# A three-stage attention and expert kernel: one step of the exact weight conversion moved from VectorE to ScalarE, and the first softmax tiles done in whole-tile instructions

## The chip, the cores and the metric

The kernel runs on one core of one Trainium2 chip. The metric is the device time of one launch in microseconds; lower is better. The engines of the core are TensorE (PE, with its weight loads as PEld), VectorE (DVE), ScalarE (ACT), GpSimd (POOL) and SyncE (SP), which issues most of the transfers.

## The reference

Three parts run one after the other on 2304 tokens. Attention with keys and values averaged over 8 positions:

```python
k_p = k.reshape(B, H, Sp, 8, D).mean(axis=3)          # B, H, S, D = 4, 8, 576, 64; Sp = 72
scores = scale * np.matmul(q, k_p.transpose(0, 1, 3, 2))
attn = np.exp(scores - np.max(scores, axis=-1, keepdims=True))
attn = attn / (np.sum(attn, axis=-1, keepdims=True) + 1e-09)
out = np.matmul(attn, v_p)
```

Then a feed-forward part in float64 weights, `y = relu(x @ w_in)**2 @ w_out`, with `w_in` 512 x 2048 and `w_out` 2048 x 512. Then a routing part: each token goes to the one of 8 experts with the largest gate logit, `relu(x @ w1) @ w2`, scaled by its gate.

## The kernel before, in words

The 2304 tokens are 9 chunks of 256 (`c` from 0 to 8). For each chunk the attention makes the input `x` of the feed-forward part, in two halves: a rounded one `xh` (ScalarE) and the rest `xl` (VectorE). Each of 16 feed-forward steps of a chunk (`g1`) is: 12 matmuls into `h` (L585), a ReLU on ScalarE (`relu`, L590), a square on VectorE or ScalarE (`square`), a rounded half `gh` on ScalarE (`high`, L601), the rest `gl` on GpSimd (`low`, L605), and 6 matmuls into `y` (L618). Chunks 0 and 1 run interleaved, one step of each by turns, and the attention of chunk 2 runs beside them.

The weights of the feed-forward part come as 64-bit floats and are converted in place as they arrive, 32 tiles of 128 x 512 (`conv(i)`). A raw tile has two 32-bit words for each number: word 1 holds the sign, the exponent and the upper bits, word 0 the lower ones. The result `cv` is put together with bits alone. Before the change:

- `sign` (VectorE, L259): `cv` = the sign bit of word 1.
- `scale` (ScalarE, L263): word 1, read as a float, times a power of two, which moves the exponent's bias.
- `merge` (VectorE, L267), twice: `cv` or word 1 shifted left by 3, then `cv` or word 0 shifted right by 29 (its top three bits).
- `high` (ScalarE, L273) writes the rounded half of the tile, `low` (GpSimd, L276) the rest.

`cv` has 4 buffers; the raw tile and the finished tile share one.

A softmax tile (`a_scores`) is up to 128 rows of 8 heads by 72 keys in two halves `a` of 4 heads. There are two forms. The whole-tile form: VectorE takes the maximum (`top`), subtracts it (`less`, L420), ScalarE does one exponential for 4 heads (`exp4`, L424), VectorE sums (L456). The head-by-head form: VectorE takes the maximum and multiplies it by a negative constant (`neg`, L409), and ScalarE does one exponential for each head with the maximum as bias and its sum as a second output (`exp`, L412, two records each). Both end with a small constant added to the sums (L428) and a reciprocal (L429) on VectorE, and a product (`norm`, L433) on GpSimd, for one tile on VectorE. Before the change the whole-tile form is used for two tiles, one of chunk 0 and one of chunk 1; the other 18 tiles go head by head.

The order of the instructions on each engine is fixed by a planner (`Steps.run`): each step has a priority, an engine and a cost in nanoseconds, and the planner takes, engine by engine, the first step of a window of 80 that could start by these costs. The costs thus decide the order of the program, and nothing else. The engines then run their own lists in order.

Of the kernel before, what the change touches and what calls it, by code (L numbers as in the profile page):

```python
# [20 lines left out]
POOL = 8  # L21
# [173 lines left out]
def tile_kernel(ctx: ExitStack, tc: tile.TileContext, q, k, v, w_in, w_out, w_gate, w1, w2, cap, gate_rows, consts, out):  # L195
# [101 lines left out]
    def k_pool(b, x, prio, load_prio, tag=None):  # L297

        buf, box = Buf("kvraw" if tag is None else tag), {}

        def load():
            box["raw"] = raw_tile(tag, f"kraw_{b}_{x}")
            nc.sync.dma_start(out=box["raw"], in_=k[b, x])

        def pool():
            nc.vector.tensor_reduce(
                out=kd[:, x], in_=box["raw"].rearrange("p (s r) -> p s r", r=POOL), axis=AX.X, op=ALU.add
            )

        add(load_prio, "SP", 840, load, w=(buf,), lat=2000)  # L310
        add(prio, "DVE", 690, pool, r=(buf, "ap"), w=(("kd", x),))

    def v_pool(b, i, prio, load_prio, tag=None):
        n = min(P, NROW - i * P)
# [66 lines left out]
    def a_scores(c, j, prio, qprio):  # L381
# [18 lines left out]
        def top(a):  # L400
            if "mx" not in box:
                box["mx"] = ap.tile([P, H], F32, tag="mx", name=f"mx_{c}_{j}", bufs=2)
                box["sm"] = ap.tile([P, H], F32, tag="sm", name=f"sm_{c}_{j}", bufs=2)
                box["ex"] = a_tile([P, H, SP], "ex", c, j, 2)
            nc.vector.tensor_reduce(out=box["mx"][:n, 4 * a:4 * a + 4], in_=box["sc", a][:n], axis=AX.X, op=ALU.max)

        def neg(a):
            m = box["mx"][:n, 4 * a:4 * a + 4]
            nc.vector.tensor_scalar_mul(out=m, in0=m, scalar1=-1.0 / 64.0)  # L409

        def exp(h):
            nc.scalar.activation(  # L412
                out=box["ex"][:n, h], in_=box["sc", h // 4][:n, h % 4], func=AF.Exp, scale=1.0 / 64.0,
                bias=box["mx"][:n, h:h + 1], accum_out=box["sm"][:n, h:h + 1],
            )
# [18 lines left out]

        st["ex", c, j] = box, ex
        add(qprio, "SP", 760 * n // P, load, w=(qT,), lat=2000)
        cells, us, tags = [], [], []
        for a in range(2):
            pool, tag = (pg, "g") if c == 2 else (pp, f"y{a}") if c < 2 and j == 1 else (pp, "sc")
# [5 lines left out]
                us.append(())  # L445
            tags.append((a, pool, tag))
        for part in [tags] if c == 2 else [tags[:1], tags[1:]]:
            add(prio(2), "PE", 480 * len(part), lambda part=part: [qk(*x) for x in part], r=(qT, ("kT", 0), ("kT", 1), "kT in", "ap"),
                w=[cells[x[0]] for x in part], u=us[part[0][0]])
        if c in DVE_SOFTMAX and (c, j) not in ACT_SOFTMAX:  # L450
            for a in range(2):
                w, u = (cells[a],), us[a]
                add(prio(3), "DVE", 370, lambda a=a: top(a), r=w, w=((mxb, a),), u=(*u, mxb, ex))
                add(prio(3), "DVE", 360, lambda a=a: less(a), r=(*w, (mxb, a)), w=((ex, a),), u=(*u, mxb, ex))
                add(prio(3), "ACT", 350, lambda a=a: exp4(a), w=((ex, a),), u=(ex,))
            add(prio(4), "DVE", 620, lambda: nc.vector.tensor_reduce(  # L456
                out=box["sm"][:n], in_=box["ex"][:n], axis=AX.X, op=ALU.add), r=((ex, 0), (ex, 1)), w=((mxb, 2),), u=(mxb, ex))
# [114 lines left out]
    def g1(c, ff, prio):  # L572
# [59 lines left out]
        add(prio + 5, "PE", 1310, mm2, r=(ghb, glb, ("W", 16 + ff, 0), ("W", 16 + ff, 1)), w=(("y", c),), u=yb)
# [909 lines left out]
```

## Time and profile before

| what | value |
|---|---|
| time, median of 3 runs | 789.33 us (787.2 to 789.95) |
| the profiled execution's time | 788.33 us |
| its span | 786.2 us, so 2.1 us lie around the span |
| TensorE busy | 702.9 us, 89% of the span |
| VectorE busy | 455.5 us, 58% |
| ScalarE busy | 317.9 us, 40% |
| GpSimd busy | 242.7 us, 31% |
| mean granted TensorE clock | 0.947 of full speed |

The shares are means over stages with different limits. The weight conversion runs from about 15 to 140 us; from there to about 540 us TensorE hardly pauses; then come the experts. The line of the profile that cuts the span into 40 slices shows this: one slice is 19.7 us.

### The profile page before, as it was taken

Reading aid. Unit: us, or ns where it says so; the run is one execution under the profiler, and the core shown is the slowest. Engines: PE = TensorE matmul, PEld = TensorE weight load, DVE = VectorE, ACT = ScalarE, POOL = GpSimd, SP = SyncE. Lnnn points to the kernel's source line nnn. Section 1 sums busy time; section 2 is a strip of 40 time slices with the busy share of each in tenths; the row PEclk is TensorE's granted clock in tenths of the full one; section 3 lists DMA queues with packets and bytes.
Section 4 is the critical chain, followed back from the end, with each engine's and each line's share of the span. In section 5 each row is a group of like instructions: output and inputs, shape, how many; then the busy total and the mean of one; then the engine's idle time right before and its main releaser. Section 6 shows DMA issues by size and latency. Waiting matters only on the chain. (4 is left out here: it accounts for less than half of the span.)

```text
span 786.2 us, 12381 instructions
## 1 busy us (share of the span) xinstructions
PE 702.9 (89%) x4231; PEld 616.0 (78%) x4232; DVE 455.5 (58%) x1181; ACT 317.9 (40%) x950; POOL 242.7 (31%) x267
## 2 busy tenths in 40 slices
PE   4788888999999999999999999997969669979993
PEld 4568676899898888888988998995949568868872
DVE  6999999322279896282696474453514412625371
ACT  3755655444343334344333433443113412624360
POOL 4476586323134233233132332221020112010240
PEclk9599999999999999999999999998888979989997
DMA  9926763210031310010100000600062611636261
GB/s 328 405 89 198 245 186 103 61 68 14 15 135 56 103 42 8 8 41 15 39 15 6 28 1 26 244 2 29 2 229 89 222 46 37 202 100 200 80 200 56
DMA packets 42597, 78.06 MB, mean 99 GB/s; under 512 B 8673, under 2 KB 18145, under 8 KB 42336
## 3 DMA queue, kind: packets, MB, share of 16 engines
q1 hardware_dynamic: 39888, 68.56, 25.9%
q0 software_dynamic: 2576, 7.93, 3.2%
q8 instruction: 58, 0.95, 0.6%
q14 instruction: 75, 0.61, 0.3%
HBM read 63.57 MB, written 13.44 MB: 98 GB/s over the span
## 5 line engine op out<-in xcount | busy, mean ns | idle before, releaser
L585 PE MATMUL h<-xh,W 128*128 128x256 f32 x1152 | 220.0, 289 | 3.1 <-DVE r L597 2.9
L605 POOL TENSOR_TENSOR gl<-r,gh 128x256 fp32r<-128x256 f32 x144 | 117.1, 814 | 277.7 <-ACT gh L601 189.6
L585 PEld LDWEIGHTS h<-xh,W 128*128 128x128 f32 x1152 | 186.3, 193 | 17.1 <-DVE r L597 6.5
L618 PE MATMUL y<-W,gh 128*128 128x512 f32 x576 | 187.9, 407 | 0.8 <-POOL W L276 0.8
L585 PE MATMUL h<-xl,W 128*128 128x256 f32 x576 | 163.7, 284 | 2.6 <-DVE xl L524 2.6
L597 DVE SCALAR_TENSOR_TENSOR r<-h,r 128x256 f32<-128x256 f32 x141 | 59.0, 418 | 112.5 <-ACT r L590 112.5
L618 PE MATMUL y<-W,gl 128*128 128x512 f32 x288 | 114.6, 398 | 0.1
L618 PEld LDWEIGHTS y<-W,gh 128*128 128x128 f32 x576 | 100.0, 191 | 17.3 <-issue 1.5
L585 PEld LDWEIGHTS h<-xl,W 128*128 128x128 f32 x576 | 111.0, 193 | 2.8 <-DVE xl L524 2.8
L1255 PE MATMUL hp<-yh,W 128*128 128x256 f32 (+1 forms) x384 | 83.7, 315 | 31.1 <-issue 31.1
L590 ACT ACTIVATE r<-h 128x256 f32<-128x256 f32 x144 | 55.2, 384 | 108.6 <-PE h L585 96.1
L601 ACT CAST gh<-r 128x256 fp32r<-128x256 f32 x144 | 58.8, 408 | 98.1 <-DVE r L597 89.9
L1255 PEld LDWEIGHTS hp<-yh,W 128*128 128x128 f32 x384 | 68.0, 210 | 36.0 <-issue 35.9
L1224 PE MATMUL po<-W,hh 128*128 128x512 f32 x224 | 71.1, 399 | 0.0
L675 DVE SCALAR_TENSOR_TENSOR junk<-ysb,wgb 128x512 bf16<-128x512 f32 x80 | 64.5, 806 | 1.9 <-ACT ysb L648 0.4
L618 PEld LDWEIGHTS y<-W,gl 128*128 128x128 f32 x288 | 54.6, 190 | 13.8 <-POOL gl L605 1.0
L267 DVE SCALAR_TENSOR_TENSOR cv<-raw,cv 128x512 int32<-128x512 int32 x64 | 62.9, 1008 | 0.4 <-ACT raw L263 0.3
L1255 PE MATMUL hp<-yl,W 128*128 128x256 f32 (+1 forms) x192 | 59.6, 311 | 2.2 <-issue 2.2
L1261 DVE SCALAR_TENSOR_TENSOR hl<-hp,hh 128x256 fp32r<-128x256 f32 x48 | 20.1, 422 | 59.6 <-ACT hh L1260 58.4
L514 PE MATMUL av<-aT,vz 128*128 128x256 f32 (+3 forms) x192 | 47.2, 379 | 8.1 <-DVE xl L524 5.5
L1213 POOL DMA_INDIRECT out_dram<-ysb,sidx x16 | 16.4, 1024 | 121.0 <-ACT ysb L1202 87.4
L276 POOL TENSOR_TENSOR W<-cv,W 128x512 fp32r<-128x512 f32 x32 | 46.4, 1459 | 21.5 <-ACT W L273 16.8
(185 smaller groups left out, 975.6 us busy)
## 6 DMA issues: line engine op xcount, KB each, us to landing
stg<-in_moe_w_dram SPq DMA_DIRECT2D x47, 512.0 KB, 4.8
raw<-in_moe_w_in_dram SPq DMA_DIRECT2D x16, 512.0 KB, 7.1
raw<-in_moe_w_out_dram SPq DMA_DIRECT2D x16, 512.0 KB, 7.4
kraw<-in_k_dram SPq DMA_DIRECT2D x16, 288.0 KB, 3.6
out_dram<-zt SPq DMA_DIRECT2D x18, 256.0 KB, 3.7
y_dram<-ysb SPq DMA_DIRECT2D x18, 256.0 KB, 2.4
qT<-in_q_dram SPq DMA_DIRECT2D x16, 256.0 KB, 3.2
vraw<-in_v_dram SPq DMA_DIRECT2D x16, 256.0 KB, 3.4
```

The costliest lines, as they stand in the source:

```text
L267: nc.vector.scalar_tensor_tensor(out=a, in0=box["raw"][:, :, word], scalar=shift, in1=a, op0=op, op1=ALU.bitwise_or)
L276: nc.gpsimd.tensor_tensor(out=W[i][:, 1], in0=f(box["a"]), in1=f(W[i][:, 0]), op=ALU.subtract)
L514: nc.tensor.matmul(ps[:, :n], vz[:m, cm].rearrange("p r d -> p (r d)"), abox["aT"][:m, blk, :n], start=(x == 0), stop=(x == 1),)
L585: nc.tensor.matmul(ps, wt[kk][:, l, o:o + P], r[:, kk, :], start=(n == 0), stop=(n == 3 * KD - 1))
L590: nc.scalar.activation(out=box["r"], in_=box["ps"], func=AF.Relu)
L597: nc.vector.scalar_tensor_tensor(out=r, in0=box["ps"], scalar=0.0, in1=r, op0=ALU.max, op1=ALU.mult)
L601: nc.scalar.copy(out=box["gh"], in_=box["r"])
L605: nc.gpsimd.tensor_tensor(out=box["gl"], in0=box["r"], in1=f(box["gh"]), op=ALU.subtract)
L618: nc.tensor.matmul(st["y", c][t], l[:, ts], r, start=(ff == 0 and n == 0), stop=(ff == NF - 1 and n == 2))
L675: nc.vector.scalar_tensor_tensor(out=junk, in0=st["yb", c, t] if c < 2 else st["ysb", c][t], scalar=1.0, in1=st["wgb"][:, e], op0=ALU.mult ...
L1224: nc.tensor.matmul(ps, l, r, start=(fi == 0 and x == 0), stop=(fi == 7 and x == 2))
L1255: nc.tensor.matmul(ps, ww[:, l, o], r[:, kk, 0:n2], start=(kk == 0 and x == 0), stop=(kk == KD - 1 and x == 2))
```

## The change

The conversion of a weight tile: `sign` is gone. A new ScalarE step `last` (L260 of the changed kernel) reads the upper 16 bits of word 0 as an unsigned integer, and scale, bias and the conversion to an integer on output leave its top three bits in `cv`. `scale` follows on ScalarE as before. VectorE then does two merges (L270), both from word 1: first the sign bit (an AND), then the shift by 3. So a tile has three VectorE instructions before and two after, and two ScalarE ones before `high` instead of one.

The softmax: all 7 tiles of chunks 0, 1 and 2 take the whole-tile form. The factor 1/64 of the scores moves into the copy that places the pooled keys (`k_place`, L347), which is an activation with a scale instead of a copy. The maximum comes out of `top` negated, so `neg` is gone everywhere. The small constant is added on ScalarE (`guard`, L427) and no more on VectorE.

The first matmuls of chunk 2's attention also depend on the last `xl` of chunk 1 (`after`). Many planner costs are changed, which moves instructions on all engines.

```diff
-DVE_SOFTMAX = (0, 1)
-ACT_SOFTMAX = ((0, 1), (1, 0))
+DVE_SOFTMAX = (0, 1, 2)
+ACT_SOFTMAX = ()
...
-        def sign():
+        def last():
+
             a = box["a"] = tp.tile([P, 512], I32, tag="cv", name=f"cv{i}", bufs=4)
-            hw = box["raw"][:, :, 1]
-            nc.vector.tensor_scalar(out=a, in0=hw, scalar1=-0x80000000, scalar2=None, op0=ALU.bitwise_and)
+            nc.scalar.activation(
+                out=a, in_=box["raw"].bitcast(U16)[:, :, 1], func=AF.Copy, scale=2.0 ** -13, bias=2.0 ** -14 - 0.5
+            )
...
-        def merge(word, shift, op):
+        def merge(x, op):
             a = box["a"]
-            nc.vector.scalar_tensor_tensor(
-                out=a, in0=box["raw"][:, :, word], scalar=shift, in1=a, op0=op, op1=ALU.bitwise_or
-            )
+            nc.vector.scalar_tensor_tensor(out=a, in0=box["raw"][:, :, 1], scalar=x, in1=a, op0=op, op1=ALU.bitwise_or)
...
-        add(prio, "DVE", 340, sign, r=(raw, "tp"), w=(cv,))
-        add(prio, "ACT", 520, scale, w=(raw,))
-        add(prio, "DVE", 605, lambda: merge(1, 3, ALU.logical_shift_left), r=(raw,), w=(cv,))
-        add(prio, "DVE", 605, lambda: merge(0, 29, ALU.logical_shift_right), r=(raw,), w=(cv,))
-        add(prio, "ACT", 525, high, r=(cv,), w=(("W", i, 0),), u=(whole,))
-        add(prio, "POOL", 1225, low, r=(cv, ("W", i, 0)), w=(("W", i, 1),))
+        add(prio, "ACT", 650, last, r=(raw, "tp"), w=(cv,))
+        add(prio, "ACT", 680, scale, w=(raw,))
+        add(prio, "DVE", 1000, lambda: merge(-0x80000000, ALU.bitwise_and), r=(raw,), w=(cv,))
+        add(prio, "DVE", 1000, lambda: merge(3, ALU.logical_shift_left), r=(raw,), w=(cv,))
+        add(prio, "ACT", 620, high, r=(cv,), w=(("W", i, 0),), u=(whole,))
+        add(prio, "POOL", 1460, low, r=(cv, ("W", i, 0)), w=(("W", i, 1),))
...
-            nc.scalar.copy(out=pairs[h, :, a], in_=kd[h])
+            nc.scalar.activation(out=pairs[h, :, a], in_=kd[h], func=AF.Copy, scale=1.0 / 64.0)
...
-            nc.vector.tensor_reduce(out=box["mx"][:n, 4 * a:4 * a + 4], in_=box["sc", a][:n], axis=AX.X, op=ALU.max)
-
-        def neg(a):
-            m = box["mx"][:n, 4 * a:4 * a + 4]
-            nc.vector.tensor_scalar_mul(out=m, in0=m, scalar1=-1.0 / 64.0)
+            nc.vector.tensor_reduce(
+                out=box["mx"][:n, 4 * a:4 * a + 4], in_=box["sc", a][:n], axis=AX.X, op=ALU.max, negate=True
+            )
...
+        def guard():
+            sm = box["sm"]
+            nc.scalar.activation(out=sm[:n], in_=sm[:n], func=AF.Copy, bias=1e-9)
+
         def recip():
             sm = box["sm"]
-            nc.vector.tensor_scalar_add(out=sm[:n], in0=sm[:n], scalar1=1e-9)
             nc.vector.reciprocal(out=sm[:n], in_=sm[:n])
...
+        after = [("xl", 1, 0, NPAIR - 1)] if c == 2 else []
```

Three places of the instruction order carry the prediction. The first is ScalarE at the start of the program, up to the first transposed attention tiles `aT`; `ex` are exponentials, `cv0` and `raw0` belong to weight tile 0. Before, the first line stands twice more for the second half of the tile:

```order
L412 ACTIVATE ex_0_1_158,sm_0_1_157<-sc_0_1_1_152,mx_0_1_156 128x72 x4
L263 ACTIVATE raw0_148<-raw0_148 128x512
L263 ACTIVATE raw1_168<-raw1_168 128x512
L273 CAST W0_223<-cv0_189 128x512
L490 COPY aT_0_0_231<-ata_0_0_214 128x4x128
L493 COPY aT_0_0_231<-atb_0_0_229 64x128
```

And after:

```order
L423 ACTIVATE ex_0_1_157<-ex_0_1_157 128x288
L427 ACTIVATE sm_0_0_134<-sm_0_0_134 128x8
L260 ACTIVATE cv0_183<-raw0_148 128x512
L423 ACTIVATE ex_0_1_157<-ex_0_1_157 128x288
L266 ACTIVATE raw0_148<-raw0_148 128x512
L260 ACTIVATE cv1_198<-raw1_166 128x512
L427 ACTIVATE sm_0_1_156<-sm_0_1_156 128x8
L266 ACTIVATE raw1_166<-raw1_166 128x512
L493 COPY aT_0_0_217<-ata_0_0_204 128x4x128
L496 COPY aT_0_0_217<-atb_0_0_213 64x128
```

The copy of `aT` stood behind the second `scale`, which waits for a VectorE `sign`; now the rows ahead of it that belong to weights wait for transfers alone, and the only VectorE results in front of it are those of the softmax.

The second place is VectorE in the same part of the program, the end of chunk 0's softmax and the first weight tiles. Before:

```order
L428 TENSOR_SCALAR sm_0_1_157<-sm_0_1_157 128x8
L429 RECIPROCAL sm_0_1_157<-sm_0_1_157 128x8
L433 TENSOR_TENSOR ex_0_1_158<-ex_0_1_158,sm_0_1_157 128x576
L267 SCALAR_TENSOR_TENSOR cv0_189<-raw0_148,cv0_189 128x512
L259 TENSOR_SCALAR cv1_210<-raw1_168 128x512
L267 SCALAR_TENSOR_TENSOR cv0_189<-raw0_148,cv0_189 128x512
L259 TENSOR_SCALAR cv2_221<-raw2_185 128x512
L267 SCALAR_TENSOR_TENSOR cv1_210<-raw1_168,cv1_210 128x512
```

And after:

```order
L270 SCALAR_TENSOR_TENSOR cv0_183<-raw0_148,cv0_183 128x512
L431 RECIPROCAL sm_0_1_156<-sm_0_1_156 128x8
L270 SCALAR_TENSOR_TENSOR cv0_183<-raw0_148,cv0_183 128x512
L435 TENSOR_TENSOR ex_0_1_157<-ex_0_1_157,sm_0_1_156 128x576
L270 SCALAR_TENSOR_TENSOR cv1_198<-raw1_166,cv1_198 128x512
L406 TENSOR_REDUCE mx_1_0_242<-sc_1_0_0_163 128x4
L270 SCALAR_TENSOR_TENSOR cv1_198<-raw1_166,cv1_198 128x512
```

The signs between the merges are gone, and with them the small addition ahead of the reciprocal.

The third place is ScalarE in the middle of the conversion, at weight tiles 22, 23 and 8. Before:

```order
L263 ACTIVATE raw22_454<-raw22_454 128x512
L263 ACTIVATE raw23_487<-raw23_487 128x512
L263 ACTIVATE raw8_518<-raw8_518 128x512
L590 ACTIVATE r_0_4_706<-h_0_4_667 128x256
L590 ACTIVATE r_1_3_718<-h_1_3_689 128x256
L601 CAST gh_0_4_723<-r_0_4_706 128x256
```

And after:

```order
L260 ACTIVATE cv22_690<-raw22_381 128x512
L604 CAST gh_1_3_695<-r_1_3_678 128x256
L266 ACTIVATE raw22_381<-raw22_381 128x512
L274 CAST W21_712<-cv21_642 128x512
L260 ACTIVATE cv23_728<-raw23_421 128x512
L423 ACTIVATE ex_2_0_706<-ex_2_0_706 64x288 x2
L593 ACTIVATE r_0_4_753<-h_0_4_715 128x256
```

Here `last` of a tile now stands ahead of `gh` and `relu` steps; it needs one of the 4 `cv` buffers, which GpSimd's `low` of an earlier tile gives back.

## Rows read from the trace of the kernel before

**Rows 1.** The page: busy time by engine, and the span in 40 slices.

```profile
PE 702.9 (89%) x4231; PEld 616.0 (78%) x4232; DVE 455.5 (58%) x1181; ACT 317.9 (40%) x950; POOL 242.7 (31%) x267
DVE  6999999322279896282696474453514412625371
```

**Rows 2.** Windows: stretch, its length, busy us of PE, PEld, DVE, ACT, POOL, granted clock, DMA.

```profile
15.00:140.00 125.00, 103.61 (x548) 85.76 (x547) 120.76 (x180) 72.26 (x199) 81.35 (x70) 0.86 0.61 210
34.00:140.00 106.00, 91.46 (x512) 77.62 (x512) 103.76 (x150) 60.86 (x162) 72.21 (x60) 0.90 0.53 176
150.00:200.00 50.00, 50.00 (x326) 45.34 (x325) 13.31 (x34) 20.24 (x73) 13.95 (x18) 1.00 0.09 32
```

**Rows 3.** Groups of lines, 15 to 140 us: busy us, mean ns, idle before.

```profile
L267 DVE SCALAR_TENSOR_TENSOR cv<-raw,cv 128x512 int32<-128x512 int32 x64 | 62.9, 1008 | 0.4 <-ACT raw L263 0.3
L259 DVE TENSOR_SCALAR cv<-raw 128x512 int32<-128x512 int32 x32 | 27.2, 867 | 0.0
L605 POOL TENSOR_TENSOR gl<-r,gh 128x256 fp32r<-128x256 f32 x23 | 23.3, 1015 | 13.8 <-ACT gh L601 8.5 <-issue 5.0 <-POOL W L276 0.3
L263 ACT ACTIVATE raw<-raw 128x512 f32<-128x512 f32 x32 | 21.4, 678 | 16.1 <-DVE cv L259 15.9 <-DMA raw<-in_moe_w_out_dram 0.2
L433 POOL TENSOR_TENSOR ex<-ex,sm 128x576 f32<-128x576 f32 (+1 forms) x5 | 6.3, 1255 | 6.7 <-ACT raw L263 4.4 <-DVE sm L429 2.3
L361 POOL TENSOR_TENSOR vz<-pv,cst 128x256 f32<-128x256 f32 (+2 forms) x9 | 6.0, 687 | 1.1 <-PE av L514 1.1
L273 ACT CAST W<-cv 128x512 fp32r<-128x512 f32 x32 | 19.8, 621 | 18.0 <-DVE cv L267 17.9
L412 ACT ACTIVATE ex<-sc,mx 64x72 f32<-64x72 f32 (+1 forms) x28 | 8.9, 320 | 2.1 <-DVE mx L409 2.1
L412 ACT ACTIVATION_READ_ACCUMULATOR ex<-sc,mx 64x1 f32 (+1 forms) x28 | 5.7, 202 | 0.0
L409 DVE TENSOR_SCALAR mx<-mx 64x4 f32<-64x4 f32 (+1 forms) x6 | 4.0, 690 | 0.0
L428 DVE TENSOR_SCALAR sm<-sm 128x8 f32<-128x8 f32 (+1 forms) x5 | 3.7, 733 | 1.1 <-ACT ex L412 1.1
L420 DVE TENSOR_TENSOR ex<-sc,mx 128x288 f32<-128x288 f32 x2 | 0.9, 443 | 0.0
L424 ACT ACTIVATE ex<-ex 128x288 f32<-128x288 f32 x2 | 0.9, 436 | 0.0
L456 DVE TENSOR_REDUCE sm<-ex 128x8 f32<-128x576 f32 x1 | 0.7, 702 | 0.0
```

**Rows 4.** Single lines, 0 to 150 us: durations in ns, shortest, median, longest.

```profile
L267 DVE SCALAR_TENSOR_TENSOR cv<-raw,cv x64: 641/684/3351, 19.3 to 136.0; 128x512 int32<-128x512 int32 x64
L259 DVE TENSOR_SCALAR cv<-raw x32: 388/524/4346, 14.9 to 130.2; 128x512 int32<-128x512 int32 x32
L276 POOL TENSOR_TENSOR W<-cv,W x32: 1257/1300/2582, 21.7 to 137.5; 128x512 fp32r<-128x512 f32 x32
L605 POOL TENSOR_TENSOR gl<-r,gh x28: 719/922/1286, 39.2 to 149.9; 128x256 fp32r<-128x256 f32 x28
L409 DVE TENSOR_SCALAR mx<-mx x10: 148/418/1228, 12.5 to 140.9; 128x4 f32<-128x4 f32 x6, 64x4 f32<-64x4 f32 x4
```

**Rows 5.** Timeline of VectorE and GpSimd, 86 to 91 us: start, duration, instruction.

```profile
87.19 0.68 DVE L267 SCALAR_TENSOR_TENSOR cv<-raw,cv 128x512 int32<-128x512 int32 x1
87.79 1.25 DVE L428 TENSOR_SCALAR sm<-sm 64x8 f32<-64x8 f32 x1
...
90.08 4.35 DVE L259 TENSOR_SCALAR cv<-raw 128x512 int32<-128x512 int32 x1
...
86.44 2.58 POOL L276 TENSOR_TENSOR W<-cv,W 128x512 fp32r<-128x512 f32 x1 [1.03 <-ACT W L273]
```

**Rows 6.** Timeline of ScalarE and TensorE, 20 to 34 us; idle before in brackets.

```profile
20.36 0.67 ACT L263 ACTIVATE raw<-raw 128x512 f32<-128x512 f32 x1 [3.41 <-DVE cv L259]
...
22.17 1.12 PE L480 MATMUL ata<-cst,ex 128*128 128x128 f32 x4 [4.29 <-ACT aT L490]
```

More of the change, by code (lines that the diff above doesn't have):

```diff
@@ L11 @@
 I32 = mybir.dt.int32
+U16 = mybir.dt.uint16
 AF = mybir.ActivationFunctionType
@@ L310, in k_pool @@
         add(load_prio, "SP", 840, load, w=(buf,), lat=2000)
-        add(prio, "DVE", 690, pool, r=(buf, "ap"), w=(("kd", x),))
+        add(prio, "DVE", 740, pool, r=(buf, "ap"), w=(("kd", x),))
     def v_pool(b, i, prio, load_prio, tag=None):
@@ L336, in v_pool @@
         else:
-            add(prio, "DVE", 610, pool, r=(buf, "ap"), w=(("v", i),))
+            add(prio, "DVE", 670, pool, r=(buf, "ap"), w=(("v", i),))
     def k_place(b, prio):
@@ L404, in top @@
                 box["ex"] = a_tile([P, H, SP], "ex", c, j, 2)
[L405 to L409 removed]
+            nc.vector.tensor_reduce(
+                out=box["mx"][:n, 4 * a:4 * a + 4], in_=box["sc", a][:n], axis=AX.X, op=ALU.max, negate=True
+            )
         def exp(h):
             nc.scalar.activation(
[L413 removed]
+                out=box["ex"][:n, h], in_=box["sc", h // 4][:n, h % 4], func=AF.Exp,
                 bias=box["mx"][:n, h:h + 1], accum_out=box["sm"][:n, h:h + 1],
@@ L419, in less @@
             m = box["mx"][:n, hs].unsqueeze(2).to_broadcast([n, 4, SP])
-            nc.vector.tensor_tensor(out=box["ex"][:n, hs], in0=box["sc", a][:n], in1=m, op=ALU.subtract)
+            nc.vector.tensor_tensor(out=box["ex"][:n, hs], in0=box["sc", a][:n], in1=m, op=ALU.add)
         def exp4(a):
             o = box["ex"][:n, 4 * a:4 * a + 4]
-            nc.scalar.activation(out=o, in_=o, func=AF.Exp, scale=1.0 / 64.0)
+            nc.scalar.activation(out=o, in_=o, func=AF.Exp)
+        def guard():
+            sm = box["sm"]
+            nc.scalar.activation(out=sm[:n], in_=sm[:n], func=AF.Copy, bias=1e-9)
         def recip():
             sm = box["sm"]
-            nc.vector.tensor_scalar_add(out=sm[:n], in0=sm[:n], scalar1=1e-9)
             nc.vector.reciprocal(out=sm[:n], in_=sm[:n])
@@ L447, in a_scores @@
         for part in [tags] if c == 2 else [tags[:1], tags[1:]]:
-            add(prio(2), "PE", 480 * len(part), lambda part=part: [qk(*x) for x in part], r=(qT, ("kT", 0), ("kT", 1), "kT in", "ap"),
+            add(prio(2), "PE", 480 * len(part), lambda part=part: [qk(*x) for x in part], r=(qT, ("kT", 0), ("kT", 1), "kT in", "ap", *after),
                 w=[cells[x[0]] for x in part], u=us[part[0][0]])
@@ L452, in a_scores @@
                 w, u = (cells[a],), us[a]
[L453 to L456, printed above, removed]
+                add(prio(3), "DVE", 440, lambda a=a: top(a), r=w, w=((mxb, a),), u=(*u, mxb, ex))
+                add(prio(3), "DVE", 450, lambda a=a: less(a), r=(*w, (mxb, a)), w=((ex, a),), u=(*u, mxb, ex))
+                add(prio(3), "ACT", 440, lambda a=a: exp4(a), w=((ex, a),), u=(ex,))
+            add(prio(4), "DVE", 740, lambda: nc.vector.tensor_reduce(
                 out=box["sm"][:n], in_=box["ex"][:n], axis=AX.X, op=ALU.add), r=((ex, 0), (ex, 1)), w=((mxb, 2),), u=(mxb, ex))
@@ L460, in a_scores @@
                 w, u = (cells[a],), us[a]
-                add(prio(3), "DVE", 370, lambda a=a: top(a), r=w, w=((mxb, a),), u=(*u, mxb, ex))
-                add(prio(3), "DVE", 75, lambda a=a: neg(a), w=((mxb, a),), u=(mxb,))
+                add(prio(3), "DVE", 440, lambda a=a: top(a), r=w, w=((mxb, a),), u=(*u, mxb, ex))
                 for h in range(4 * a, 4 * a + 4):
-                    add(prio(3), "ACT", 296, lambda h=h: exp(h), r=(*w, (mxb, a)), w=((ex, a), (mxb, 2)), u=(*u, mxb, ex))
-        add(prio(4), "DVE", 230, recip, w=((mxb, 2),), u=(mxb,))
+                    add(prio(3), "ACT", 522, lambda h=h: exp(h), r=(*w, (mxb, a)), w=((ex, a), (mxb, 2)), u=(*u, mxb, ex))
+        add(prio(4), "ACT", 210, guard, w=((mxb, 2),), u=(mxb,))
+        add(prio(4), "DVE", 200, recip, w=((mxb, 2),), u=(mxb,))
         if (c, j) in NORM_DVE:
-            add(prio(4), "DVE", 620, lambda: norm(nc.vector), r=((mxb, 2),), w=((ex, 0), (ex, 1)), u=(mxb, ex))
+            add(prio(4), "DVE", 740, lambda: norm(nc.vector), r=((mxb, 2),), w=((ex, 0), (ex, 1)), u=(mxb, ex))
         else:
-            add(prio(4), "POOL", 1110, lambda: norm(nc.gpsimd), r=((mxb, 2),), w=((ex, 0), (ex, 1)), u=(mxb, ex))
+            add(prio(4), "POOL", 1260, lambda: norm(nc.gpsimd), r=((mxb, 2),), w=((ex, 0), (ex, 1)), u=(mxb, ex))
     def a_trans(c, j, aTb, abox, o, prio):
@@ L622, in g1 @@
         wr = [("W", 4 * (ff // 4) + kk, l) for kk in range(KD) for l in range(2)]
-        add(prio, "PE", 1310, mm, r=(*xcells[c], *wr, *(("tp",) if c == 2 else ())), w=(hb,), u=(xb,))
-        add(prio + 1, "ACT", 270, relu, r=(hb,), w=(rb,))
+        add(prio, "PE", 1390, mm, r=(*xcells[c], *wr, *(("tp",) if c == 2 else ())), w=(hb,), u=(xb,))
+        add(prio + 1, "ACT", 380, relu, r=(hb,), w=(rb,))
         if act_square:
-            add(prio + 1, "ACT", 310, square, w=(rb,))
+            add(prio + 1, "ACT", 420, square, w=(rb,))
         else:
-            add(prio + 1, "DVE", 340, square, r=(hb,), w=(rb,))
-        add(prio + 1, "ACT", 310, high, r=(rb,), w=(ghb,))
-        add(prio + 1, "POOL", 690, low, r=(rb, ghb), w=(glb,))
+            add(prio + 1, "DVE", 415, square, r=(hb,), w=(rb,))
+        add(prio + 1, "ACT", 405, high, r=(rb,), w=(ghb,))
+        add(prio + 1, "POOL", 900, low, r=(rb, ghb), w=(glb,))
         yb = ybs[c]
-        add(prio + 5, "PE", 1310, mm2, r=(ghb, glb, ("W", 16 + ff, 0), ("W", 16 + ff, 1)), w=(("y", c),), u=yb)
+        add(prio + 5, "PE", 1390, mm2, r=(ghb, glb, ("W", 16 + ff, 0), ("W", 16 + ff, 1)), w=(("y", c),), u=yb)
     ybufs = {0: Buf("y"), 1: Buf("y")}
```

## The prediction

> **What bounds the kernel now.** I read the page's busy shares and slices first [rows 1]. TensorE is busy 89% of the span, so the question is where its missing time lies. From slice 2 to slice 7 (20 to 138 us) VectorE stands at 9 tenths, and it falls to 3 as soon as the conversion is over. The chain of work that ended last is of no use here, since it holds only the final GpSimd store. So I cut the span into stretches [rows 2]. From 150 to 200 us TensorE is busy 50.00 of 50.00 us at clock 1.00 and VectorE needs 13.31: there TensorE is the bound. From 15 to 140 us it is the other way round: VectorE is busy 120.76 of 125.00 us, TensorE 103.61 at a mean clock of 0.86. Whatever shortens the conversion stretch starts the full TensorE stretch earlier by the same amount; nothing else in the diff can be worth more than a few microseconds.
>
> But a busy VectorE is not a working one. The groups of that stretch [rows 3] give a merge 1008 ns in the mean, a sign 867; the single lines [rows 4] give a merge 684 in the median, a sign 388 at its shortest. The rest is waiting that counts as busy. The timeline shows for what [rows 5]. GpSimd's `low` starts at 86.44 and takes 2.58 us, though its shortest is 1.257: it gets on only when VectorE's merge, which would take the next 0.60 us from 87.19, is through at 87.79, and then ends at 89.02. VectorE's tiny addition starts at 87.79 and lasts 1.25 us, until 89.04, though an instruction of that kind takes as little as 148 ns [rows 4]. The sign of 4.35 us at 90.08 is the extreme case. So merges, signs and these small instructions on one side and GpSimd's subtractions on the other take turns on something both need.
>
> The Trainium skill, in "SBUF — State Buffer", section "Who interferes with whom", names it: a VectorE instruction with two SBUF inputs, or in a two-port mode, and a GpSimd instruction that reads SBUF lock each other out of one shared port, and issue order decides who waits. By that rule a removed sign is worth only the time that it holds the port, 12.4 us in all, while by the busy rows it is worth 27.2; the turns in the timeline agree with the rule.
>
> **How full the shared thing is.** Before, in the 125 us: 64 merges at 0.684 are 43.8 us, 32 signs at 0.388 are 12.4 [rows 4]. On GpSimd 32 `low` at 1.257 are 40.2 and 23 `gl` at 0.719 are 16.5 [rows 3, 4]. That is 112.9 of 125.0 us. GpSimd's 14 other products of the stretch come on top with 6.3 + 6.0 us [rows 3], some of that waiting. So the turns are full or nearly so, and this, not VectorE's own work, is the limit.
>
> **The change, part by part.**
> The **sign** goes: 27.2 us of VectorE busy time in the stretch, of which 32 x 0.388 = 12.4 its own and 14.8 waiting. **neg** and the **small addition** go: 4.0 + 3.7 = 7.7 us busy [rows 3], of which 11 x 0.148 = 1.6 their own and 6.1 waiting. The merges stay 64; an AND in place of a shift, the same two operands and shapes, so I give them the same 0.684.
>
> **Added on VectorE**: 28 head-by-head exponentials in the stretch are 3.5 tiles that turn into the whole-tile form; each adds two `less` at 0.443 and one sum at 0.702 [rows 3], 1.59 us, together 5.6 us. Maxima out of PSUM are there before as after.
>
> So VectorE falls by 27.2 + 7.7 - 5.6 = 29.3 us if every wait goes with its instruction, and by 12.4 + 1.6 - 5.6 = 8.4 us if all waiting moves to the merges that are left. By the shared turns the stretch falls by the 12.4 us that the signs held, provided that the softmax work finds room beside GpSimd's turns. The truth should be between 8.4 and 12.4: GpSimd still needs its turns in full, so its subtractions go on stopping VectorE, and 29.3 would need them not to. I take the middle, **10.4 us**.
>
> **Added on ScalarE**: 32 `last`. No row has one; the nearest are `scale`, which also reads words with a gap (678), and `high` (621) [rows 3]: 19.9 to 21.7 us, I take the latter. The 28 exponentials with their second records go, 8.9 + 5.7 = 14.6 us; 7 `exp4` at 0.436 add 3.1, some 5 `guard` at 0.20 to 0.32 (the small record and the small exponential) 1.3. Net +11.5 us, so 72.26 becomes some 84 of 115 us: room is there. ScalarE stood idle before `scale` for VectorE's sign 15.9 us and before `high` for the merges 17.9 [rows 3], and the first of these waits has no cause any more. If that cover were gone, the 11.5 us would be the price. The scale inside the key copy replaces one instruction by one of the same shape, at nothing, under the same cover.
>
> The Trainium skill, in "ScalarE: Activation LUTs", section "Rules for kernel authors", advises VectorE for additions and multiplications; row by row it is right, 0.388 on VectorE against 0.678 here. By that rule the change would cost 32 x 0.29 = 9.3 us of engine time more. It speaks of an engine by itself; here VectorE's time is what lacks, so I keep it as the rival on ScalarE below.
>
> **The start.** At 20.36 us ScalarE has stood 3.41 us for the second sign, and behind it stands the copy of `aT`, for which TensorE waits 4.29 us [rows 6]. In the changed order no weight step ahead of that copy waits for VectorE. Up to 3.4 us of this can come off the first matmuls; it is part of the 10.4, not beside it, as the signs of that time are in the sum.
>
> **The rest.** In chunks 3 to 8 the head-by-head form stays, `neg` goes and the addition moves to ScalarE: one hop more of 0.20 to 0.32 us for each of 13 tiles, hidden by an attention that runs a chunk ahead while TensorE is full; if it were not hidden, 13 x 0.3 = 4 us. On SP's queue the loads of batch 1's values and the writes of zeros to the output move behind or between the last raw weight loads; ScalarE waited 0.2 us in all for a weight transfer [rows 3] and the transfer engines are 53% busy from 34 to 140 us [rows 2], so I give it nothing. The planner's new costs move few rows on TensorE behind the conversion; nothing.
>
> **Sum.** 788.33 us (the profiled execution: 786.2 span and 2.1 around it) less 10.4 is 777.9; the median of the runs shown is 1.0 us above the profiled one, so I say 778 us.
>
> **Rivals.**
> *TensorE becomes the bound.* If the turns loosen so much that the rest of TensorE's pauses vanish, the gain ends where TensorE is full. From 34 to 140 us it idles 106.00 - 91.46 = 14.5 us [rows 2], and 3.4 us come from the start: 17.9 us, 770.4. For it: the planner's costs are now near the rows (1000 for a merge, 650 for `last`), so the lists may fit better. Against: GpSimd's 40.2 + 16.5 us still alternate with 43.8 us of merges. A gain in clock (0.90 now) could add a little.
> *ScalarE takes a part back.* Its list is in order, and `last` and `scale` stand ahead of `gh` and `relu`. If half of the 11.5 us falls on TensorE's path, the gain is 10.4 - 5.8 = 4.6 us, 784.
> *It does nothing.* The whole 11.5 us on the path against 10.4: 788 to 789. The skill's rule above would end here.
> *Slower.* `last` needs a `cv` buffer, and before, the sign that took it never stood idle for one (0.0 in its row [rows 3]). On ScalarE such a wait would hold the `gh` and `relu` behind it. If ScalarE waits half a `low`, 0.63 us, for each of 28 tiles, 17.6 us less 10.4 make 795.5. It decides only when a buffer is held longer than four tiles' pace, 4 x 125/32 = 15.6 us; at the start tile 0 goes from its sign at 14.9 to the end of its `low` at about 23.0 (the first of each, [rows 4]), 8.1 us. So I hold it unlikely.
>
> **How the numbers follow.** Within 0.3% (2.4 us) a measurement of this kernel can hardly tell a change from none. Forecast, 776 to 781: 0.48. TensorE full, about 770: 0.20. ScalarE takes half, 781 to 786.5: 0.17. Nothing: 0.08. Slower: 0.07. The first three are faster: 0.85. For 8 in 10 the range leaves out the slower case, the nothing and a rest below the TensorE case: 768.5 to 786.5.
>
> **What would show it.** In the conversion stretch: merges still 64, with a mean that stays above 0.684, so that waiting has moved and not gone; VectorE still the fullest engine; the stretch that ends with the last weight at 140 us now ending near 130; `last` at 0.62 to 0.68 us; the copy of `aT` some 3 us earlier; ScalarE no longer waiting for a sign; the stretch of full TensorE as long as before. Wrong would be: merges near 0.684 in the mean (then the gain is larger), ScalarE's idle time ended by GpSimd's `low` (then `cv` is the new wait), or any difference of more than 2 us behind 150 us.

## The result and the profile after

The changed kernel takes 762.22 us (median of 4 runs, 760.34 to 762.67) against 789.64 us before (787.2 to 789.97): a ratio of 0.9655, interval 0.9629 to 0.968. It is faster, as said, but by 27 us where 11 were forecast, and below the lower end of the range. The profiled execution took 762.46 us, its span is 760.5.

The page of the changed kernel: busy time by engine, then TensorE and VectorE in 40 slices, which answer to [rows 1].

```profile
PE 690.2 (91%) x4231; PEld 606.6 (80%) x4232; DVE 425.4 (56%) x1108; ACT 328.8 (43%) x932; POOL 247.9 (33%) x267
...
PE   3899999999999999999999999996959399969993
...
DVE  6899898222798962824972933542516122635271
```

TensorE runs the same 4231 matmuls in 12.7 us less of busy time, so they have not only moved closer together: they have become shorter.

To see where, I cut both spans at the same events: the first feed-forward matmul, the moment when ScalarE starts to copy out chunk 0's `y`, and a late `y`, 2412 matmuls further on in both. The columns are those of [rows 2]. Before:

```profile
0.00:33.69 33.69, 17.97 (x58) 13.65 (x59) 26.24 (x49) 15.56 (x51) 13.84 (x25) 0.80 0.98 358
33.69:164.01 130.32, 115.78 (x663) 99.08 (x663) 110.61 (x168) 71.44 (x200) 79.12 (x69) 0.92 0.46 151
164.01:543.07 379.06, 373.56 (x2412) 331.17 (x2411) 225.63 (x705) 151.24 (x530) 112.90 (x138) 1.00 0.14 45
543.07:786.20 243.13, 195.54 (x1102) 172.11 (x1100) 93.00 (x259) 79.67 (x170) 36.84 (x35) 0.90 0.37 121
```

After:

```profile
0.00:28.24 28.24, 15.00 (x59) 12.08 (x60) 19.02 (x34) 14.59 (x32) 11.67 (x23) 0.88 0.97 350
28.24:137.37 109.13, 106.11 (x663) 91.53 (x663) 97.03 (x150) 80.57 (x190) 86.06 (x71) 1.00 0.61 200
137.37:518.67 381.30, 375.07 (x2412) 332.29 (x2411) 216.38 (x666) 153.72 (x543) 113.36 (x138) 1.00 0.14 44
518.67:760.50 241.83, 193.98 (x1102) 170.75 (x1100) 92.99 (x259) 79.93 (x170) 36.81 (x35) 0.89 0.37 122
```

The first two rows hold the whole gain, 5.45 + 21.19 = 26.6 us; behind them 2.2 us are lost and 1.3 won. The second row holds the same 663 matmuls in both kernels. **Seen from TensorE**, its pauses there fall from 130.32 - 115.78 = 14.54 us to 3.02, by 11.5; and its busy time falls by 9.7, since the granted clock rises from 0.92 to 1.00 (115.78 x 0.92 = 106.5). **Seen from VectorE**, in both rows together it is busy 20.8 us less (136.85 to 116.05) and idle 5.8 us less (27.2 to 21.3). The two views add up to the same 26.6 us.

The groups of the changed kernel's conversion stretch, 15 to 130 us, in the columns of [rows 3]:

```profile
L270 DVE SCALAR_TENSOR_TENSOR cv<-raw,cv 128x512 int32<-128x512 int32 x64 | 70.6, 1125 | 0.0
L277 POOL TENSOR_TENSOR W<-cv,W 128x512 fp32r<-128x512 f32 x32 | 48.2, 1513 | 11.2 <-ACT W L274 10.8
...
L266 ACT ACTIVATE raw<-raw 128x512 f32<-128x512 f32 x32 | 21.5, 676 | 0.0
L260 ACT ACTIVATE cv<-raw 128x512 int32<-128x512 uint16 x32 | 21.2, 669 | 2.9 <-POOL W L277 2.3 <-DMA raw<-in_moe_w_in_dram 0.6
L274 ACT CAST W<-cv 128x512 fp32r<-128x512 f32 x32 | 19.8, 620 | 6.6 <-DVE cv L270 6.3
...
L459 DVE TENSOR_REDUCE sm<-ex 128x8 f32<-128x576 f32 (+1 forms) x6 | 4.5, 743 | 1.4 <-ACT ex L423 1.4
L419 DVE TENSOR_TENSOR ex<-sc,mx 128x288 f32<-128x288 f32 (+1 forms) x10 | 4.3, 443 | 0.0
```

Merges took on 7.7 us of waiting (62.9 in [rows 3], 70.6 now), while the signs, `neg` and the small addition took 27.2 + 7.7 us with them. `last` takes 669 ns, within the bounds of its estimate, and waits 2.3 us for a `cv` buffer. The single lines, as in [rows 4]:

```profile
L270 DVE SCALAR_TENSOR_TENSOR cv<-raw,cv x64: 673/1041/3225, 16.4 to 121.3; 128x512 int32<-128x512 int32 x64
```
```profile
L277 POOL TENSOR_TENSOR W<-cv,W x32: 1274/1580/1759, 20.1 to 124.3; 128x512 fp32r<-128x512 f32 x32
```

The last `low` ends near 125.8 us, where it ended near 138.8: 13.0 us earlier, near the 12.4 that the signs held by the turns. That the sum by turns comes this near is luck, since most of the waiting did not move to the merges as it supposed. About the time it was wrong: the conversion's end was not what TensorE waited for. These are TensorE's waits before, from the first feed-forward matmul until chunk 0 is out (in total, times, longest):

```profile
PE ata L480 <- POOL ex L433: 5.8, 2, 2.9
PE h L585 <- DVE xl L524: 2.6, 1, 2.6
PE av L514 <- DVE xl L524: 2.3, 2, 2.0
PE h L585 <- DVE r L597: 1.7, 3, 0.9
PE av L514 <- ACT aT L490: 1.3, 1, 1.3
PE y L618 <- POOL W L276: 0.8, 1, 0.8
```

Of 14.5 us only 0.8 are for a weight. The rest is for small attention and feed-forward steps that stand on VectorE, GpSimd and ScalarE in line with the conversion. After the change the two longest are:

```profile
PE h L588 <- POOL W L277: 1.0, 2, 0.7
PE av L517 <- DVE xl L527: 0.7, 1, 0.7
```

What such a wait costs beyond itself stands in the timeline of TensorE before (start, duration, idle before in brackets):

```profile
57.42 0.40 PE L585 MATMUL h<-xh,W 128*128 128x256 f32 x2
60.39 0.39 PE L585 MATMUL h<-xl,W 128*128 128x256 f32 x1 [2.58 <-DVE xl L524]
...
61.47 0.63 PE L585 MATMUL h<-xh,W 128*128 128x256 f32 x2
62.11 0.63 PE L585 MATMUL h<-xh,W 128*128 128x256 f32 x2
```

Soon after the pause of 2.58 us the same pair of matmuls takes 0.63 instead of 0.40 us; the granted clock there is 0.50, the lower of the two levels (1.2 and 2.4 GHz). After the change the clock is 1.00 in every stretch of 10 us from 30 us to the end of chunk 0; before, it is below 1.00 in seven of the ten from 30 to 130 us. Not all of that belongs to the pauses of this stretch, since the clock was low when it began:

```profile
33.69:36.00 2.31, 2.31 (x12) 2.31 (x12) 1.76 (x5) 2.20 (x8) 0.30 (x1) 0.50 1.05 420
36.00:38.00 2.00, 2.00 (x14) 2.00 (x14) 1.97 (x5) 1.58 (x5) 1.05 (x2) 0.69 1.02 410
```

By these two rows an estimated 2.31 x 0.50 + 2.00 x 0.31 = 1.8 of the 9.7 us come from the low clock of the start.

### The profile page after: what moved, and what is told of

Its sections match the earlier page's. It is cut to its first block, busy times and chain, and to the rows that moved or that the text cites. A ratio compares the mean times of both kernels' runs of the same rounds, so it can differ in the third digit from the quotient of the medians.

```text
span 760.5 us, 12240 instructions
## 1 busy us (share of the span) xinstructions
PE 690.2 (91%) x4231; PEld 606.6 (80%) x4232; DVE 425.4 (56%) x1108; ACT 328.8 (43%) x932; POOL 247.9 (33%) x267
## 5 line engine op out<-in xcount | busy, mean ns | idle before, releaser
L588 PE MATMUL h<-xh,W 128*128 128x256 f32 x1152 | 216.0, 286 | 3.9 <-DVE r L600 2.9
L608 POOL TENSOR_TENSOR gl<-r,gh 128x256 fp32r<-128x256 f32 x144 | 120.3, 837 | 264.1 <-ACT gh L604 179.6
L588 PEld LDWEIGHTS h<-xh,W 128*128 128x128 f32 x1152 | 183.8, 190 | 16.0 <-DVE r L600 4.2
L600 DVE SCALAR_TENSOR_TENSOR r<-h,r 128x256 f32<-128x256 f32 x141 | 59.0, 418 | 106.5 <-ACT r L593 106.3
L621 PEld LDWEIGHTS y<-W,gh 128*128 128x128 f32 x576 | 99.0, 189 | 17.3 <-issue 1.9
L588 PEld LDWEIGHTS h<-xl,W 128*128 128x128 f32 x576 | 109.4, 190 | 0.0
L270 DVE SCALAR_TENSOR_TENSOR cv<-raw,cv 128x512 int32<-128x512 int32 x64 | 70.6, 1125 | 0.0
L678 DVE SCALAR_TENSOR_TENSOR junk<-ysb,wgb 128x512 bf16<-128x512 f32 x80 | 66.2, 828 | 1.6
L277 POOL TENSOR_TENSOR W<-cv,W 128x512 fp32r<-128x512 f32 x32 | 48.2, 1513 | 11.2 <-ACT W L274 10.8
L1263 ACT ACTIVATE hh<-hp 128x256 fp32r<-128x256 f32 x48 | 18.4, 384 | 76.9 <-PE hp L1258 76.1
```

What stands on the lines that cost most here:

```text
L270: nc.vector.scalar_tensor_tensor(out=a, in0=box["raw"][:, :, 1], scalar=x, in1=a, op0=op, op1=ALU.bitwise_or)
L588: nc.tensor.matmul(ps, wt[kk][:, l, o:o + P], r[:, kk, :], start=(n == 0), stop=(n == 3 * KD - 1))
L600: nc.vector.scalar_tensor_tensor(out=r, in0=box["ps"], scalar=0.0, in1=r, op0=ALU.max, op1=ALU.mult)
L608: nc.gpsimd.tensor_tensor(out=box["gl"], in0=box["r"], in1=f(box["gh"]), op=ALU.subtract)
L621: nc.tensor.matmul(st["y", c][t], l[:, ts], r, start=(ff == 0 and n == 0), stop=(ff == NF - 1 and n == 2))
L678: nc.vector.scalar_tensor_tensor(out=junk, in0=st["yb", c, t] if c < 2 else st["ysb", c][t], scalar=1.0, in1=st["wgb"][:, e], op0=ALU.mult ...
```

## The experiments

Each job ran the kernel before beside its kernels; it took 787.39, 787.81 and 787.89 us there, about 2 us less than beside the changed kernel. The changed kernel did not run in these jobs, so a difference of 2 us against its 762.22 says nothing; e5, which differs from it in a few costs alone, took 762.3 there. Diffs are against the changed kernel where nothing else is said.

**Which part is it?** e1 has only the conversion's part, with its costs; e2 only the softmax's, with the scaled key copy and `after`, which were not tried by themselves; e5 has both, but the old costs of the feed-forward and pooling steps.

Of the change, e1 leaves out this, with all that belongs to it:

```diff
+DVE_SOFTMAX = (0, 1)
+ACT_SOFTMAX = ((0, 1), (1, 0))
-DVE_SOFTMAX = (0, 1, 2)
-ACT_SOFTMAX = ()
```

e2 leaves out this:

```diff
-        add(prio, "ACT", 650, last, r=(raw, "tp"), w=(cv,))
+        add(prio, "DVE", 340, sign, r=(raw, "tp"), w=(cv,))
```

And e5 leaves out only this and its like:

```diff
-        add(prio + 1, "ACT", 405, high, r=(rb,), w=(ghb,))
+        add(prio + 1, "ACT", 310, high, r=(rb,), w=(ghb,))
```

> Only the weight conversion is changed (last on ScalarE, two merges, their new costs); the softmax and all other costs are as before. If the gain comes from VectorE time taken away in front of the steps that feed TensorE, the sign's 27.2 us make this the larger part: 770 to 776 us. If the head-by-head exponentials and the tiny VectorE instructions were what held TensorE, 784 to 789. If only the new order matters, 780 or more.

> Only the softmax is changed (whole-tile form for chunks 0 to 2, negated maximum, guard on ScalarE, their new costs); the conversion keeps its sign on VectorE. If the sign's waiting is what matters, 780 to 787 us. If the softmax is as much worth as the conversion, 773 to 779.

> The whole change but for the planner costs of the feed-forward steps and of the pooling, which stay as before; the conversion and the softmax have their new costs. If the costs of the converted steps carry the order's part, 760 to 765 us as the changed kernel. If the feed-forward costs (each 30% higher in the changed kernel) carry it, 770 to 778.

e1: 778.14 us, 0.9885 (0.9843 to 0.9927). e2: 782.88, 0.9936 (0.9913 to 0.9959). e5: 762.3, 0.9695 (0.9659 to 0.9731). Alone the parts give 9.2 and 4.5 us, together 25.5: each is worth more with the other. The costs that e5 leaves out are worth nothing that can be measured. e1 missed the 770 to 776 that were expected of it; e2 and e5 lie within theirs.

**Is it the order?** e4 has the changed instructions with all the costs of before. e3 and e6 have the instructions of before with the new costs, e6 without the new cost of an exponential. In e9 only the merge has its old cost; in e10 merge and `low` have costs nearer to their measured means.

In e4 (and, of these, only the merges in e9; in e10 they have 1125 and `low` 1510):

```diff
-        add(prio, "ACT", 650, last, r=(raw, "tp"), w=(cv,))
+        add(prio, "ACT", 520, last, r=(raw, "tp"), w=(cv,))
...
-        add(prio, "DVE", 1000, lambda: merge(-0x80000000, ALU.bitwise_and), r=(raw,), w=(cv,))
+        add(prio, "DVE", 605, lambda: merge(-0x80000000, ALU.bitwise_and), r=(raw,), w=(cv,))
```

In e3 and e6, against the kernel before:

```diff
-        add(prio, "DVE", 605, lambda: merge(1, 3, ALU.logical_shift_left), r=(raw,), w=(cv,))
+        add(prio, "DVE", 1000, lambda: merge(1, 3, ALU.logical_shift_left), r=(raw,), w=(cv,))
```

> The instructions are those of before; only the planner's costs are set to the new values wherever the step exists. If the gain is in what the instructions do, this is within 4 us of before: 785 to 793 us. If it is the order that the costs make, 765 to 778.

> All instructions of the changed kernel, but the planner's costs of before. If the order matters little, 760 to 765 us. If the new costs carry a good part, 770 to 780.

> The instructions of before with the new costs, but the head-by-head exponential keeps its old cost of 296, since with 522 it was placed ahead of the transposes of chunk 0. If costs near the measured durations make a better order by themselves, 774 to 783 us. If they do not help without the shorter instructions, 786 to 792.

> The changed kernel with one planner cost put back: a merge at 605 instead of 1000, so that the lists are made as if merges did not wait. If the squares and the second halves of x are late because the planner puts too many merges ahead of them, this costs most of the 12.5 us that separate the old costs from the new: 768 to 776 us. If it is another cost that counts, 760 to 765.

> The changed kernel with the costs of the contended steps set to their new measured means: merge 1125 and low 1510 instead of 1000 and 1460. TensorE is already full from 45 us on, so 759 to 764 us; anything above 768 would say that the order is a matter of luck more than of right costs.

e3: 805.59 us, 1.0229 (1.0183 to 1.0275); one transposition stands 34.6 us for an exponential that the order puts late, an accident of this mixture. e6: 790.33, 1.0048 (1.0031 to 1.0065). e4: 774.86, 0.9833 (0.979 to 0.9876). e9: 768.51, 0.9743 (0.969 to 0.9796). e10: 770.56, 0.9778 (0.9725 to 0.983).

So the order by the new costs gives nothing or a loss with the old instructions, and 774.86 - 762.22 = 12.6 us with the new ones. Costs nearer to the means (e10) are 8.3 us worse; by the expectation above, more than 768 us means luck in the order more than right costs. e3 lies above both of its ranges; e9 lies in its 768 to 776, but one cost put back loses only half of the 12.6 us, and not most of it. What the order does between e4 and the changed kernel is seen on VectorE: it waits in `square` (`r`) for the ReLU. The same wait in e4, then in the changed kernel, each from the first feed-forward matmul until chunk 0 is out:

```profile
DVE r L600 <- ACT r L593: 18.1, 10, 2.8
```
```profile
DVE r L600 <- ACT r L593: 6.0, 6, 2.4
```

TensorE feels it: in e4 it waits for those squares, and in the changed kernel no such wait is listed. The line of e4:

```profile
PE h L588 <- DVE r L600: 5.5, 3, 3.2
```

Two kernels do not fit this reading. In e6 the same wait falls to 8.3 us from the 13.9 before, and chunk 0 is out 5.4 us earlier; but the 2412 matmuls that follow take 384.87 us instead of 379.06, which takes it back. In e10 the wait is shorter than in the changed kernel, and VectorE idles as long; there the merges wait longer, a mean of 1200 ns instead of 1125:

```profile
DVE r L600 <- ACT r L593: 4.8, 8, 1.0
```
```profile
L270 DVE SCALAR_TENSOR_TENSOR cv<-raw,cv 128x512 int32<-128x512 int32 x64 | 75.5, 1200 | 0.0
```

So the order also moves the waiting in the turns. In e4 VectorE works nearly as little as in the changed kernel, and stands waiting for the rest:

| kernel | chunk 0 out at | VectorE busy until then | idle | of it `square` for ReLU | time |
|---|---|---|---|---|---|
| before | 164.01 | 136.85 | 27.2 | 13.9 | 789.64 |
| e1, conversion alone | 153.67 | 115.62 | 38.1 | 18.9 | 778.14 |
| e2, softmax alone | 158.01 | 134.33 | 23.7 | 10.0 | 782.88 |
| e4, old costs | 153.22 | 119.51 | 33.7 | 18.1 | 774.86 |
| e6, new costs alone | 158.62 | 133.98 | 24.6 | 8.3 | 790.33 |
| e10, merge at 1125 | 142.96 | 121.62 | 21.3 | 4.8 | 770.56 |
| e9, old cost of a merge | 142.82 | 115.06 | 27.8 | 11.3 | 768.51 |
| changed | 137.37 | 116.05 | 21.3 | 6.0 | 762.22 |

**What is an instruction of the shared turns worth?** These keep the order of the changed kernel, row by row, and add 32 instructions to VectorE's conversion, at the same place: e8 issues the first merge twice, e12 sums one word plane instead, an instruction with a single input. e7 moves `low` from GpSimd to VectorE, and so takes GpSimd out of the conversion; its order differs.

In e8:

```diff
-        add(prio, "DVE", 1000, lambda: merge(-0x80000000, ALU.bitwise_and), r=(raw,), w=(cv,))
+        add(prio, "DVE", 1000, lambda: [merge(-0x80000000, ALU.bitwise_and) for _ in range(2)], r=(raw,), w=(cv,))
```

In e12, issued right behind the same merge:

```diff
+            nc.vector.tensor_reduce(
+                out=d, in_=f(box["raw"][:, :, 1]).rearrange("p (s r) -> p s r", r=8), axis=AX.X, op=ALU.add
+            )
```

In e7:

```diff
-        add(prio, "POOL", 1460, low, r=(cv, ("W", i, 0)), w=(("W", i, 1),))
+        add(prio, "DVE", 700, low, r=(cv, ("W", i, 0)), w=(("W", i, 1),))
```

> The changed kernel with the AND merge issued twice (it changes no bit the second time); the order is otherwise the same. It adds 32 instructions of 0.68 us that take turns with GpSimd, more than the signs held. If the sum of the turns sets the time, as forecast, about 19 us come back: 778 to 785. If the turns have slack and TensorE is the bound, less than half of that: 763 to 771.

> The changed kernel with one more VectorE instruction for each weight tile at the place of the third merge of the run before, of about the same length, but a sum that reads one tile only (no row of such a sum in the trace is ever held up by GpSimd); its result is used nowhere. If a third merge is dear because it takes turns with GpSimd, this costs clearly less than the 26.7 us: 765 to 777. If plain VectorE time is what is short, it costs about as much: 782 to 790.

> The changed kernel with the second half of each weight tile (low) subtracted on VectorE and not on GpSimd, at a planner cost of 700. If merges wait for GpSimd's subtractions, their mean falls from 1125 to below 850 ns and the 32 added subtractions at 0.68 us take the place of the waiting: VectorE's busy time in the stretch stays within 8 us and the time is 757 to 770. If the merges are slow for another reason, their mean stays above 1000 ns, VectorE gets 22 us more, and the time is 775 or more.

e8: 788.96 us, 1.0021 (1.0 to 1.0042), 26.7 us above the changed kernel: 32 instructions take the whole gain back, where 778 to 785 us were expected. e12: 771.74, 0.9777 (0.9727 to 0.9827), 9.5 us above it and within its 765 to 777. The groups of e8 from 15 to 150 us, then of e12:

```profile
L270 DVE SCALAR_TENSOR_TENSOR cv<-raw,cv 128x512 int32<-128x512 int32 x96 | 100.3, 1060 | 1.1
```
```profile
L270 DVE SCALAR_TENSOR_TENSOR cv<-raw,cv 128x512 int32<-128x512 int32 x64 | 63.4, 1003 | 0.0
...
L274 DVE TENSOR_REDUCE dm<-raw 128x64 f32<-128x512 f32 x32 | 21.5, 673 | 0.0
```

The third merge adds 29.7 us to VectorE's merges, 0.93 each and not the 0.684 that one holds [rows 4]: the wait comes with the instruction. The sums add 21.5 us of their own, and the merges' waiting falls by 7.2: 14.3 net. So 26.7 us of time for 29.7 of VectorE, and 9.5 for 14.3. VectorE's idle time until chunk 0 is out changes little in either, 17.0 us in e8 and 18.3 in e12.

e7: 772.21, 0.9818 (0.98 to 0.9836), slower than the changed kernel. Merges average 842 ns instead of 1125, so much of what held them up was `low` on GpSimd (`gl` and the softmax products are left there); the time misses the 757 to 770 that were to go with this. `low` takes 784 on VectorE where it takes 1513 on GpSimd, but VectorE is busy 101.03 us from 15 to 130, hardly less than 104.52.

**What bounds the start?** e11 puts 10 matmuls on an unused bank into TensorE's pause at 18 us; nothing else moves.

```diff
+            if c == 0 and j == 0:
+                fl = pp.tile([P, CH], F32, tag="h", name="fill", bufs=2)
+                for _ in range(10):
+                    nc.tensor.matmul(fl[:, 0:144], ident, kT[:, 0:144], start=True, stop=True)
```

> The changed kernel with 10 matmuls, 128 by 144, into an unused bank between the transposes of the two first attention tiles, where TensorE idles for 3.1 us; their result is used nowhere. If it is the pause that takes the clock down to 0.66 in the next 10 us, the first 16 value matmuls run at full speed and TensorE reaches its first feed-forward matmul 1 to 3 us earlier: 759 to 761 us. If the weights are what the start waits for, or the clock falls all the same, 762 to 764.

e11: 761.48 us, 0.9651 (0.961 to 0.9692), not to be told from the changed kernel, and between its two ranges. The clock from 20 to 30 us rises from 0.66 to 1.00, so the pause did take it down. The first feed-forward matmul comes at 27.86 instead of 28.24 us, though in this trace the first transposes, ahead of the added matmuls, happened to start 1.05 us later (17.36 instead of 16.31). Soon after it TensorE waits for a weight:

```profile
22.78 3.27 PE L521 MATMUL av<-aT,vz 128*128 128x256 f32 x12 [0.84 <-ACT aT L497]
...
30.26 0.39 PE L592 MATMUL h<-xh,W 128*128 128x256 f32 x1 [0.95 <-POOL W L277]
```

In the changed kernel the same attention products and the first feed-forward matmuls are:

```profile
21.92 6.39 PE L517 MATMUL av<-aT,vz 128*128 128x256 f32 x16 [0.46 <-ACT aT L493]
28.24 0.50 PE L588 MATMUL h<-xh,W 128*128 128x256 f32 x2
```

There too TensorE waits for weights soon after, 1.0 us in two waits. Chunk 0 is out at 135.98 instead of 137.37 us in e11, and both spans are 760.5: a faster TensorE at the start gains nothing that the time shows. Why what follows takes as much longer was not followed.

## Why the prediction was wrong

**The path of the sum failed**: "Whatever shortens the conversion stretch starts the full TensorE stretch earlier by the same amount." The conversion ended 13.0 us earlier and chunk 0 was out 26.6 us earlier, and TensorE was full long before the conversion ended:

```profile
50.00:110.00 60.00, 60.00 (x384) 52.76 (x384) 55.00 (x79) 45.78 (x106) 50.26 (x43) 1.00 0.71 221
```

Before, TensorE had waited for small attention and feed-forward steps on the engines that the conversion shares; of 14.5 us only 0.8 were for a weight.

**So did the choice within the sum**: "The truth should be between 8.4 and 12.4: GpSimd still needs its turns in full, so its subtractions go on stopping VectorE, and 29.3 would need them not to." VectorE's busy time until chunk 0 is out fell by 20.8 us; the bounds by rows and by turns were 29.3 and 8.4. The waiting removed was 14.8 + 6.1 = 20.9 us by the prediction's own terms; 7.7 of it moved to the merges, 13.2 went. Per instruction the wait stayed about what it was: before, the 107 merges, signs and small instructions had 19.1 + 14.8 + 6.1 = 40.0 us beyond their own time, 0.37 each; after, 64 merges have 70.6 - 43.8 = 26.8, 0.42 each; in e8, 96 have 34.6, 0.36 each. (It is no constant: with 64 merges it is 0.31 in e12, where sums stand between them, and 0.50 in the order of e10.) GpSimd still stops VectorE, but each instruction fewer is one fewer to be stopped. e8 shows the price in time: 26.7 us for 32. e12 shows that instructions outside the turns, as many and as long, cost a third of that at the same place.

The Trainium skill, in "SBUF — State Buffer", section "Who interferes with whom", says that a `tensor_reduce` never contends with GpSimd on this chip; the trace of e12 agrees, 32 of them took 668 to 679 ns. The rule that was cited in the prediction from there, an exclusive lock, stands too: without `low` on GpSimd the merges of e7 took 842 ns instead of 1125. That a removed sign is worth only the time for which it holds the lock was drawn from it and is not in it.

**The largest miss is the price of the order**: "The planner's new costs move few rows on TensorE behind the conversion; nothing." It measured 12.6 us, in the conversion stretch and not behind it. With the old costs the new instructions give 787.39 - 774.86 = 12.5 us, close to the 10.4 forecast. But that is no confirmation of the sum: in e4 VectorE's work fell by 17.3 us, and its idle time rose by 6.5, most of it in `square` waiting for the ReLU. The new costs win 12.4 us of idle time back, 12.1 of them in that wait, and 12.6 us of time. The table says the same of e1: less work, more idling. That fits with the parts being worth more together. That this wait is the cause between e4 and the changed kernel is read from rows and not shown: no run took it away by itself, and in e10 the time is 8.3 us longer with a shorter wait.

**A rival was mis-sized.** "TensorE becomes the bound" had the right mechanism at a chance of 0.20. Its 14.5 us of idle and 3.4 of start, 17.9, came out as 11.5 + 5.45 = 17.0. What it left out is the clock, "a gain in clock could add a little": 9.7 us. 788.33 - 17.0 - 9.7 + 0.9 (what follows behind chunk 0) = 762.5, the measured 762.46. The clock could have been priced from the trace of before: the stretch from 34 to 140 us ran at 0.90 [rows 2], so its 91.46 us of busy time held some 9 us that a full clock would not need.

**Right were**: TensorE's pauses as the place of the gain, VectorE as what fed them late; merges above 0.684 in the mean; the end of the conversion (125.8 us against "near 130"); `last` at 669 ns; ScalarE no longer waiting for a sign; the stretch of full TensorE behind it nearly unchanged (379.06 and 381.30, the 2.2 us are just above the 2 that were allowed). Not so was "VectorE still the fullest engine": from 15 to 130 us TensorE is fuller, 107.42 us against 104.52.

```profile
15.00:130.00 115.00, 107.42 (x648) 91.24 (x646) 104.52 (x160) 89.14 (x206) 91.42 (x77) 0.97 0.67 230
```

The copy of `aT` came 4.1 us earlier (3 said):

```profile
17.40 0.56 ACT L493 COPY aT<-ata 128x512 f32<-128x512 f32 x1
```

The slower rival fell: `last` waited 2.3 us for a buffer where 17.6 were priced. What ScalarE took back cannot be seen in the whole change; in e1, where the head-by-head exponentials stay and ScalarE is busy 103.10 us until chunk 0 is out instead of 95.17, TensorE waits 8.7 us for weights and `gl`, so that rival may have a place without the softmax's part.

**Open** stays why single costs act as they do (e9 loses half of the order's worth, e10 more than that), and how far the new order was found by fortune. The sum of the pauses does not set the clock: e8 pauses 20.1 us in its stretch at a clock of 0.97, before 14.5 at 0.92. No kernel that was run is clearly faster than the changed one.

## What to carry to other kernels

When one engine's instructions wait for another's in turns, price a removed one at its own time and most of its waiting (here 13.2 of 20.9 us went), and check the price by adding the same number back with the order kept. Ask first whom TensorE waits for, row by row, and not which engine is fullest; then price the clock beside the pauses, since the matmuls behind a pause are longer too. Where a table of costs sets the order, run the old costs with the new instructions before you give the table nothing.

## What was not expected of the hardware

- Beside pauses of 14.5 us spread over 130 us TensorE lost another 9.7 us by the clock, an estimated 1.8 of it by the low clock that it began with. The Trainium skill, in "TensorE: Matmul & The Clock Gate", section "What's actually happening", says that the gate follows how busy the engine has been; e11 agrees, 10 matmuls in a pause hold the clock at 1.00 where it was 0.66.
- A VectorE instruction in the turns waits 0.36 to 0.42 us in the mean whether there are 96, 64 or 107 of them in the stretch (e8, the changed kernel, before); with 64 merges it is 0.31 where sums stand between them (e12) and 0.50 in another order (e10).
